# Recurrent cells at 4/3 of their pace beside a tiled feed-forward, and a first product in three float32r parts for the last two token groups

## The chip, the cores and the metric

The kernel runs on one core of a Trainium2 chip. The metric is the device time of one execution in microseconds. The engines are TensorE (PE; its weight loads are listed apart as PEld), VectorE (DVE), ScalarE (ACT), GpSimd (POOL) and SyncE (SP), which here only issues DMAs.

## The reference

An mLSTM cell runs over 768 tokens for 4 batches of 8 heads with head dimension 40. Its output, laid out as 3072 tokens of 320 values, goes through a feed-forward block with a leaky ReLU. All is float32.

```python
for t in range(S):                                   # S = 768, state C: 40x40 a head, n: 40
    m_new = max(f_gate[t] + m, i_gate[t])
    f_stab, i_stab = exp(f_gate[t] + m - m_new), exp(i_gate[t] - m_new)
    C = f_stab * C + i_stab * outer(v[t], k[t])
    n = f_stab * n + i_stab * k[t]
    y[t] = sigmoid(o_gate[t]) * (C @ q[t]) / max(abs(n . q[t]), 1)
x = y as (4 * 768, 320)
h = x @ w_in                                          # 320 -> 2048
out = max(0.01 * h, h) @ w_out                        # 2048 -> 320
```

## The kernel before

**Cells.** The 768 tokens are cut into six chunks of 128. A cell is one chunk of one batch; cell s is batch s % 4 of chunk s // 4, so there are 24. Cells of chunks 2 to 5 take two units on TensorE: `u_parts(s)` (scores of q and k and the state's additions into banks `sd`, L614 and L619; the scores are multiplied by the gate weights w on VectorE, L624, and the state gets its addition, L596) and `u_mix(s)` (one product `pT` with values and state, L695; then on VectorE transposes, a denominator, the output gate, on GpSimd L592 and L709, and a transpose L713; the result goes to a DRAM scratch `x_dr`, L716). Before `u_parts` the cell's w must be there: the gate sums of a chunk are written to the DRAM scratch `a_dr` and spread over partitions by a DMA (`spread`, L413; a second spread `ea` for q, L421), then GpSimd adds a causal mask (`prep_mask`, L450), then ScalarE takes 8 exponentials (`prep_exp`, L458). `ahead(s)` prepares k and q (loads of `rb`, L398, VectorE L505 and L511), the state (L592) and the scaled keys (L478). `feed(s + 4)`, called behind `u_mix(s)`, asks for the k, v and w of the cell that takes over its tiles (L356, L359, L413).

**Feed-forward.** A group is the 512 tokens of one chunk in all batches; there are groups 0 to 5. `gather_x` brings `x_dr` into `xT` (L730). The first product makes 16 tiles of 128 hidden units by 512 tokens, in eight pairs. A pair runs two tiles side by side on the two 64-row halves of TensorE, in five slots of 64 input rows each (L759, 10 matmuls of 512 columns); ScalarE applies the leaky ReLU on the way to `acts` (L767). The second product uses seven block products in place of eight, for two halves n, 14 products of 8 matmuls with 160 columns (L835), in the order p1, p2, p6, p7, p4, p5, p3, each for both n. The results are combined by VectorE (L853, L858, L862, L870, L887, L892), ScalarE (L854, L867, L875, L881) and GpSimd (L868, L876, L882): p4's result is added on GpSimd (L882), p5's and p3's on VectorE (L887, L892). PSUM has four banks for the products (`psf`) and four for the cells (`psc`).

**Order.** The order on TensorE, VectorE, ScalarE and GpSimd is written out by hand. Beside group g's feed-forward units (16 for the first product, 14 for the second) stand the cells of chunk g + 1, at fixed unit numbers:

```python
pairs = (2, 2, 6, 6, 14, 14, 19, 19, 19)     # u_parts x2, u_mix x2, u_parts x2, u_gates, u_mix x2
masks = {0: (2, 3), 12: (4, 5)}              # prep_mask of cells c * 4 + n ahead of unit 0 and 12
```

All DMAs but a few at the start are issued by SP, in an order made by the framework. Each engine works off its list in order, and a wait holds what is behind it. Tiles of the cells (`kn`, `qn`, `S`, `rb`, `xb` and the work tiles) live in the same pools as the rest for the whole run. `narrow_weights` (L247 to L263) works on raw weights at the start; its rows are prices of single VectorE operations.

Of the kernel before, what the change touches and what calls it, by code (L numbers as in the profile page):

```python
# [9 lines left out]
F32 = mybir.dt.float32  # L10
U32 = mybir.dt.uint32
U64 = mybir.dt.uint64
# [6 lines left out]
def kernel(  # L19
# [58 lines left out]
    dr = ctx.enter_context(tc.tile_pool(name="dr", bufs=1, space=bass.MemoryType.DRAM))  # L78

# [39 lines left out]
    kn = consts.tile([P, NL, H, DP], F32, name="kn")  # L119
    qn = consts.tile([P, NL, H, DP], F32, name="qn")  # L120
    S_t = [consts.tile([P, 2, H, DP], F32, name=f"S{n}") for n in range(NL)]
    S_v = [t[:].rearrange("p u h (k d) -> p u h k d", d=QW) for t in S_t]
    rb_t = [consts.tile([P, 3, RW], F32, name=f"rb{n}") for n in range(NR)]
    xb = consts.tile([P, PR * TB, QW], F32, name="xb")
# [147 lines left out]
    def gates(c):  # L272
# [5 lines left out]
        F = wk.tile([n, P], F32, name="F", bufs=1)  # L278
        nc.vector.tensor_tensor_scan(F[:], fc, zeros[:n].to_broadcast([n, P]), 0.0, op0=ALU.add, op1=ALU.add)
        if c > 0:  # L280
            il_t = wk.tile([BH, P], F32, name="il", bufs=1)
            nc.vector.tensor_scalar(il_t[:], il, scalar1=m0[:], scalar2=None, op0=ALU.subtract)
            il = il_t[:]
        m = wk.tile([n, P], F32, name="m", bufs=1)
        nc.vector.tensor_tensor_scan(m[:], fc, il, -1e30 if c == 0 else 0.0, op0=ALU.add, op1=ALU.max)
        a = wk.tile([n, P], F32, name="a", bufs=1)
        nc.vector.tensor_tensor(a[:], F[:], m[:], op=ALU.subtract)
        bu = wk.tile([BH, 3, P], F32, name="bu", bufs=1)
# [13 lines left out]
    def gates_exp(c):  # L302
# [9 lines left out]
        if c > 0:  # L312
            nc.sync.dma_start(a_dr[c, 0].rearrange("u n t -> n u t"), a[:].rearrange("n (u t) -> n u t", u=2))
            if c > 1:
                nc.sync.dma_start(a_dr[c, 1].rearrange("u n t -> n u t"), bu[:, 2, :].rearrange("n (u t) -> n u t", u=2))
            if 1 < c < NB - 2:
                load_fi(c + 2)
# [25 lines left out]

    def load(s):
# [11 lines left out]
        nc.sync.dma_start(d["k"][:, :, :D], k[b, :, rows, :].rearrange("h p d -> p h d"))  # L356
        for u in range(2):
            for i in range(2):
                nc.sync.dma_start(  # L359
                    S_v[n][ts(u, SL), u, :, i, :DB],  # L360
                    v[b, :, c * P + u * SL : c * P + (u + 1) * SL, DB * i : DB * (i + 1)].rearrange("h p d -> p h d"),
                )
# [42 lines left out]

    def spread(s):
# [3 lines left out]
        w = wk.tile([P, H, P], F32, name="w", bufs=NL)  # L410
        d["w"] = w[:].rearrange("p h t -> p (h t)")[:, : H * SL].rearrange("p (h t) -> p h t", t=SL)
        for u in range(2):
            nc.sync.dma_start(d["w"][ts(u, SL)], a_dr[c, 0, u, b * H : (b + 1) * H, :].partition_broadcast(SL))  # L413

    def spread_q(s):
# [3 lines left out]
        d["ea"] = wk.tile([P, H, SL], F32, name="ea", bufs=EAB)  # L419
        for r in range(2):  # L420
            nc.sync.dma_start(  # L421
                d["ea"][ts(r, SL)], a_dr[c, 1, 1 - r, b * H : (b + 1) * H, :].partition_broadcast(SL),
            )

    def spread_first(a, s2):
# [12 lines left out]
        for n in range(2):  # L438
            w = st[s2 + n]["w"] = wk.tile([P, H, P], F32, name="w", bufs=NL)
# [20 lines left out]
    def prep_vu(s):  # L460
# [3 lines left out]
        if s < NS:  # L464
            d["vu"] = wk.tile([P, H, 2, V1], F32, name="vu")
# [34 lines left out]
    def prep_kq(s):  # L500

        d = st[s]
        d["kqT"] = wk.tile([P, 2, PR * P], F32, name="kqT")
# [20 lines left out]
    def u_split(s):  # L524

        d = st[s]
        d["kqT"] = wk.tile([P, 2, PR * P], F32, name="kqT")
# [14 lines left out]
    def u_transpose(s):  # L542
        d = st[s]
        d["kqT"] = wk.tile([P, 2, PR * P], F32, name="kqT")
# [92 lines left out]
    def u_values(s):  # L637
# [4 lines left out]
        d["den"] = wk.tile([P, H], F32, name="den")  # L642
        denominators(d["den"][:], pa[:, :, D])

    def gate(s):

        d = st[s]
        d["x"] = wk.tile([P, Dm], F32, name="x")
# [7 lines left out]
    def u_plain(s):  # L656
# [13 lines left out]
        den = wk.tile([P, H], F32, name="den")  # L670
        denominators(den[:], hN[:, :, 0, DB])
        if b < 2:
            d["x"] = wk.tile([P, Dm], F32, name="x")[:]
# [10 lines left out]
    def u_mix(s):  # L684
# [16 lines left out]
        hb = wk.tile([P, PR * TB, QW], F32, name="hb", bufs=1)  # L701
        nc.vector.transpose(hb[:].rearrange("p (j n) d -> p j n d", n=TB), in_blocks(pT[:]))  # L702
        den = wk.tile([P, PR * TB], F32, name="den")
# [8 lines left out]
        xq = wk.tile([P, PR * P], F32, name="x")  # L712
# [6 lines left out]
    def gather_x(s):  # L719

        c, b = divmod(s, B)
        if ("xT", c) not in st:
            st["xT", c] = wk.tile([P, KC, GT], F32, name="xT", bufs=1)
        xT = st["xT", c]
        src = x_dr[s].rearrange("(k p) t -> p k t", p=DP)
        for r in range(2):
            at = 0
            while at < KC:
                k0, n = run_of(r, at)
                nc.sync.dma_start(xT[DP * r : DP * (r + 1), at : at + n, ts(b, P)], src[:, k0 : k0 + 2 * n - 1 : 2, :])  # L730
                at += n

# [20 lines left out]
    def ff_units(g):  # L753
        xT = st["xT", g]
# [59 lines left out]
        return firsts + fast_units(g)  # L814
# [104 lines left out]
    def ahead(s):  # L919

        if s < NS:
            if s < 2 * B:
# [99 lines left out]
    with tc.manual_schedule(engines={E.PE, E.DVE, E.Activation, E.Pool}):  # L1022
# [20 lines left out]
        for c in range(1, NB + 1):  # L1043
            if c > 1:
                ffs = ff_units(c - 1)
            cells = cell_units(c) if c < NB else []
            n_ff, n_c = len(ffs), len(cells)
            done = fed = 0
            waiting, after = [], []
            for i in range(n_ff):  # L1050
                if c == 1:
                    run(now, 2 if i < 10 else 3 if i < 14 else 4)
                    for n in fetch.get(i, ()):
                        load_weights(QN + n)
                    if i == 0:
                        prep_mask(B)
                        ahead(B)
                        load_fi(3)
                for s, steps in lazy.items():
                    if s in late and late[s] > 0:  # L1060
                        late[s] -= 1
                    else:
                        run(steps, 3)
                for n in masks.get(i, ()) if 1 < c < NB else ():
# [70 lines left out]
```

## Time and profile before

| | us |
|---|---|
| median of 3 runs (lowest, highest) | 511.85 (510.85, 513.27) |
| span of the profiled execution | 508.0 |
| the runs' median over that span (what lies around it) | 3.85 |
| PE busy | 492.0 |
| DVE, ACT, POOL busy | 308.1, 171.5, 137.7 |
| DMA queue of SP, share of 16 DMA engines | 52.2% |

The times come from executions that are not profiled; the page and the trace are of one profiled execution. Busy times are unions of an engine's instructions; DMA issues are not counted as busy, neither on SP nor on ACT. In a row by stage the columns are PE, PEld, DVE, ACT, POOL (busy us, instructions), the granted TensorE clock, the DMA share and GB/s. In the chain of waits each line has its start, its length and what it is; in a timeline, start, length, engine, line, operation, and in brackets the idle time before it and who ended it.

### The profile page before, as it was taken

The page shows a single profiled execution, that of the slowest core. Times are in us where ns is not written, and L with a number is a line of the kernel's source. Part 1 is how long each engine was busy: PE and PEld are TensorE (multiplying, and loading weights), DVE is VectorE, ACT ScalarE, POOL GpSimd, SP SyncE. Part 2 cuts the span into 40 slices and gives each one's busy share as a digit, 9 for nine tenths or more (in the row PEclk, how much of TensorE's full clock was granted, in tenths as well). Part 3 has the DMA queues.
Part 4 walks back from the last instruction along what each step waited for, and adds up shares of the span by engine and source line. Part 5 has one row for each costly group of instructions (what it writes and reads, how often), then busy time and mean ns, then how long its engine had stood idle before and what let it go on. Part 6 is the DMA issues. An engine that isn't in the chain of part 4 may idle for free.

```text
span 508.0 us, 12526 instructions
## 1 busy us (share of the span) xinstructions
PE 492.0 (97%) x4981; PEld 366.6 (72%) x4981; DVE 308.1 (61%) x515; ACT 171.5 (34%) x478; POOL 137.7 (27%) x175
## 2 busy tenths in 40 slices
PE   8878999999999999999999999999899999999997
PEld 7766878767655489955589855599755599744797
DVE  4779898899954778635765826764825664101321
ACT  3664864652722510323411323311213411022210
POOL 4243443360402404413104614014612003000020
PEclk9877999999999999999999999999999999999999
DMA  9977687888765551565663566564466212200001
GB/s 116 146 204 154 149 219 185 168 152 175 155 145 87 131 124 46 133 130 144 147 132 92 115 137 170 137 141 97 109 135 177 68 53 62 69 1 1 1 1 52
DMA packets 165290, 59.21 MB, mean 117 GB/s; under 512 B 128816, under 2 KB 156016, under 8 KB 165232
## 3 DMA queue, kind: packets, MB, share of 16 engines
q1 hardware_dynamic: 164848, 58.28, 52.2%
q8 instruction: 39, 0.64, 0.5%
q14 instruction: 19, 0.16, 0.1%
q10 hardware_dynamic: 384, 0.13, 0.1%
HBM read 51.68 MB, written 6.70 MB: 115 GB/s over the span
## 4 chain that ended last, share of the span: by engine, by line
PE 79%; DVE 9%; DMA 3%; ACT 3%; POOL 2%; issue 2%; SPq 2%; ACTq 0%; POOLq 0%; DVEq 0%
PE ph L759 36%; PE po L835 26%; PE po L794 6%; PE pT L695 3%; PE sd L614 3%; SPq L359 1%; PE sd L619 1%; DMA S<-in_v_dram 1%; ACT kqT L540 1%; PE tkq L548 1%; DVE raw L261 1%; DMA rb<-in_q_dram 1%; DMA w<-a_dr 1%; PE pa L641 1%; DVE qn L511 1%
## 5 line engine op out<-in xcount | busy, mean ns | idle before, releaser
L759 PE MATMUL ph<-xT,w_in 64*128 64x512 f32 (+1 forms) x1120 | 216.2, 538 | 2.4 <-DVE y L887 1.4
L759 PEld LDWEIGHTS ph<-xT,w_in 64*128 64x128 f32 x1120 | 108.6, 189 | 95.1 <-issue 86.3
L767 ACT ACTIVATE acts<-ph 128x512 f32<-128x512 f32 (+1 forms) x112 | 53.9, 533 | 179.0 <-PE ph L759 178.9
L835 PEld LDWEIGHTS po<-w_out,acts 128*128 128x128 f32 x640 | 87.3, 190 | 3.8 <-issue 3.8
L835 PE MATMUL po<-w_out,acts 128*128 128x160 f32 x640 | 89.1, 300 | 0.0
L450 POOL TENSOR_TENSOR w<-w,i 128x512 f32<-128x512 f32 x20 | 26.9, 1345 | 117.3 <-DMA w<-a_dr 117.2
L624 DVE TENSOR_TENSOR qn<-w,sd 64x512 f32<-64x512 f32 x40 | 27.4, 684 | 40.2 <-PE sd L619 20.5
L458 ACT ACTIVATE w<-w,gT 128x64 f32<-128x64 f32 (+1 forms) x192 | 50.8, 348 | 2.7 <-POOL w L450 1.7
L592 POOL TENSOR_TENSOR S<-S,f 40x336 f32<-40x336 f32 x36 | 32.0, 889 | 67.3 <-PE pT L695 36.3
L835 PE MATMUL po<-raw,acts 128*128 128x160 f32 x320 | 45.5, 300 | 0.0
L835 PEld LDWEIGHTS po<-raw,acts 128*128 128x128 f32 x320 | 43.9, 190 | 0.3
L794 PE MATMUL po<-w_out,acts 128*128 128x320 f32 x128 | 36.5, 436 | 0.0
L702 DVE STREAM_TRANSPOSE hb<-pT 128x512 f32<-128x512 f32 x16 | 11.5, 717 | 31.0 <-PE pT L695 30.8
L794 PEld LDWEIGHTS po<-w_out,acts 128*128 128x128 f32 x128 | 23.6, 190 | 9.3 <-issue 0.3
L511 DVE TENSOR_TENSOR qn<-kqT,ea 64x512 f32<-64x512 f32 x32 | 28.4, 888 | 1.0
L709 POOL TENSOR_TENSOR xb<-xb,den 128x320 f32<-128x320 f32 x16 | 11.7, 729 | 56.8 <-DVE xb L706 56.6
L596 DVE TENSOR_TENSOR S<-S,sd 40x336 f32<-40x336 f32 x36 | 18.1, 503 | 12.1 <-POOL S L592 11.2
L614 PEld LDWEIGHTS sd<-kqT 40*64 40x64 f32 x640 | 19.9, 135 | 6.1 <-issue 6.1
L822 DVE TENSOR_TENSOR raw<-acts 128x1024 f32<-128x1024 f32 x10 | 11.8, 1222 | 18.3 <-ACT acts L767 18.2
L713 DVE STREAM_TRANSPOSE x<-xb 128x512 f32<-128x512 f32 x16 | 18.2, 1140 | 7.6 <-POOL xb L709 7.6
L835 PE MATMUL po<-raw 128*128 128x160 f32 x160 | 22.5, 299 | 0.0
L835 PEld LDWEIGHTS po<-raw 128*128 128x128 f32 x160 | 22.0, 190 | 0.0
(151 smaller groups left out, 551.8 us busy)
## 6 DMA issues: line engine op xcount, KB each, us to landing
w<-a_dr SPq DMA_DIRECT2D x40, 128.0 KB
rb<-in_k_dram SPq DMA_DIRECT2D x64, 80.0 KB
rb<-in_q_dram SPq DMA_DIRECT2D x64, 80.0 KB
rb<-in_o_gate_dram SPq DMA_DIRECT2D x64, 80.0 KB
ea<-a_dr SPq DMA_DIRECT2D x32, 128.0 KB
kn<-in_k_dram SPq DMA_DIRECT2D x24, 160.0 KB
raw<-in_moe_w_out_dram SPq DMA_DIRECT2D x6, 640.0 KB
S<-in_v_dram SPq DMA_DIRECT2D x80, 40.0 KB
```

What stands on the lines that cost most here:

```text
L450: nc.gpsimd.tensor_tensor(w, w, cm2.unsqueeze(1).to_broadcast([P, H, SL]), op=ALU.add)
L458: yield nc.scalar.activation(w[:, h, :], w[:, h, :], AF.Exp, bias=gT[c][:, 0, bh : bh + 1], scale=1.0)
L511: nc.vector.tensor_tensor(mixed(s)[rows, 1 - r], d["kqT"][rows, 1].rearrange("p (h t) -> p h t", t=SL), d["ea"][rows], op=ALU.mult,)
L592: nc.gpsimd.tensor_tensor(new, old, g, op=ALU.mult)
L596: nc.vector.tensor_tensor(new, new, st[s]["dC", u], op=ALU.add)
L614: nc.tensor.matmul(bank[1 - u][toks, h, :], lhsT=kqT[rows, 0, ts(h, SL)], rhs=kqT[rows, 1, ts(h, SL)], start=True, stop=True,)
L624: nc.vector.tensor_tensor(mixed(s)[toks, u], w[toks], bank[1 - u][toks], op=ALU.mult)
L713: nc.vector.transpose(in_blocks(xq[:]), xb[:].rearrange("p (j n) d -> p j n d", n=TB))
L759: nc.tensor.matmul(ph[r][:, cols], lhsT=w_row(r, slot, j), rhs=xT[DP * r : DP * (r + 1), slot, cols], start=(slot == 0), stop=(slot == KC ...
L767: nc.scalar.activation(acts[:, f, cols], ph[r][:, cols], AF.Prelu, alpha=0.01)
L794: nc.tensor.matmul(po[n][:], lhsT=acts[:, f, ts(n, P)], rhs=w_out[:, f, :], start=(f == 0), stop=(f == NF - 1),)
L835: nc.tensor.matmul(bank[:], lhsT=left[:, f, :], rhs=right[:, f, :], start=f == 0, stop=f == KH - 1)
```

## The change

- The cells run by a clock of ticks, 30 a group, that goes on at 4/3 of a tick for each feed-forward unit. `pairs` and `masks` now count in ticks. Chunk 2 still begins at unit 2 of group 1; the last mix, of chunk 5, comes at unit 22 of group 3 in place of unit 19 of group 4.
- For cells of chunks 3 to 5, k and the four parts of v are asked for by ScalarE, one or two a unit, and so are all gathers of x. `spread` and `spread_q` are one DMA each in place of two.
- The cells' tiles have pools of their own, which are closed behind the last mix. In their place come three versions of `w_in` (the raw bits, a low part scaled by 2^12, and a combination of both), and the same of x.
- Group 4 from its third pair on and all pairs of group 5 make the first product as three float32r products (raw, low, dif) and combine them. The parts are made in 20 steps, two or three a unit, from unit 22 of group 3 on; those of group 5's x during group 4's second product.

```diff
-        for u in range(2):
-            nc.sync.dma_start(d["w"][ts(u, SL)], a_dr[c, 0, u, b * H : (b + 1) * H, :].partition_broadcast(SL))
+        spread_rows(d["w"], a_dr[c, 0, :, b * H : (b + 1) * H, :])
...
+        def bring(eng):
+            eng.dma_start(d["k"][:, :, :D], k[b, :, rows, :].rearrange("h p d -> p h d"))
+            yield
+            for u in range(2):
+                for i in range(2):
+                    eng.dma_start(
+                        S_v[n][ts(u, SL), u, :, i, :DB],
+                        v[b, :, c * P + u * SL : c * P + (u + 1) * SL, DB * i : DB * (i + 1)].rearrange("h p d -> p h d"),
+                    )
+                    yield
+        if c < 3:
+            for _ in bring(nc.sync):
+                pass
+        else:
+            later[s] = [bring(nc.scalar), 5]
...
-                nc.sync.dma_start(xT[DP * r : DP * (r + 1), at : at + n, ts(b, P)], src[:, k0 : k0 + 2 * n - 1 : 2, :])
+                nc.scalar.dma_start(xT[DP * r : DP * (r + 1), at : at + n, ts(b, P)], src[:, k0 : k0 + 2 * n - 1 : 2, :])
...
+    def open_parts():
+        cells_stack.close()
+        kp = ctx.enter_context(tc.tile_pool(name="kp", bufs=1))
...
+    def split_w_parts(n, half):
+        at = ts(half, WC // 2)
+        src = w_in[:, n, at]
+        held = []
+        def first():
+            t = tmp_part()[:].rearrange("p k t -> p (k t)")
+            held.append(t)
+            top_bits(t, src)                                        # VectorE, 128x640, & 0xFFFFF000
+            nc.gpsimd.tensor_tensor(t, t, src, op=ALU.subtract)
+        def second():
+            t = held[0]
+            nc.vector.scalar_tensor_tensor(
+                parts["w", "dif"][n][:, at], in0=t, scalar=1.0 + 1.0 / EPS, in1=src, op0=ALU.mult, op1=ALU.add,
+            )
+            nc.scalar.activation(parts["w", "low"][n][:, at], t, AF.Copy, scale=1.0 / EPS)
+        return first, second
+    def split_x(s):
...
+        top_bits(t, src)
+        nc.vector.tensor_tensor(low, t, src, op=ALU.subtract)
+        nc.vector.scalar_tensor_tensor(
+            parts["x", "dif"][:, :, cols], in0=low.bitcast(F32), scalar=1.0 + 1.0 / EPS, in1=src, op0=ALU.mult, op1=ALU.add,
+        )
...
+        def triple(j):                                              # rows(): 5 slots x 2 halves, float32r
...
+            def first():
+                ph.extend(psf.tile([P, GT], F32, name=f"ph{r}", tag="mm") for r in range(2))
+                rows(j, ph, "raw", True, False)
+            def second():
+                rows(j, ph, "low", False, True)
+            def third():
+                pe.extend(psc.tile([P, GT], F32, name=f"pe{r}", tag="c") for r in range(2))
+                rows(j, pe, "dif", True, True)
+                fs = [acts[:, f_of(r, j), :] for r in range(2)]
+                for r in range(2):
+                    nc.scalar.activation(fs[r], pe[r][:], AF.Copy, scale=-EPS)
+                for r in range(2):
+                    nc.vector.scalar_tensor_tensor(
+                        fs[r], in0=ph[r][:], scalar=1.0 + EPS, in1=fs[r], op0=ALU.mult, op1=ALU.add,
+                    )
+                for r in range(2):
+                    nc.scalar.activation(fs[r], fs[r], AF.Prelu, alpha=0.01)
...
+            order = [steps[0][0], steps[1][0], steps[0][1], steps[2][0], steps[1][1], steps[3][0], steps[2][1], xs[0], xs[1]]
+            order += [steps[4][0], steps[3][1], xs[2], xs[3]]
+            for m in range(5, len(steps)):
+                order += [steps[m][0], steps[m - 1][1]]
+            return order + [steps[-1][1]]
...
+        for g in range(1, NB):
+            firsts, seconds = three_units(g, LEAD if g == THREE[0] else 0) if g in THREE else ff_units(g)
+            ffs = firsts + seconds
+            at.update(group=g, past=False)
+            for i in range(len(ffs)):
+                at["past"] = i >= len(firsts) - 1
+                upto = min(ENDS + 1, (TICKS * (g - 1) + i + 1) * 4 // 3)
+                for m in range(t, upto):
+                    before_tick(m)                                  # exponentials, masks
                 ffs[i]()
...
+                for m in range(t, upto):
+                    after_tick(m)                                   # cells, ahead, load_late, feed
+                gather()
+                if t <= ENDS < upto:
+                    open_parts()
+                    for n in range(QN):
+                        fetch_w_part(n)
+                    todo = split_steps()
+                t = max(t, upto)
+                bring_later(1 if i < len(firsts) else 2)
+                prepare(3 if i < len(firsts) else 2)
+                if g + 1 < NB and g in THREE and i in range(len(firsts) + 4, len(firsts) + 12, 2):
+                    split_x((g + 1) * B + (i - len(firsts) - 4) // 2)
```

## The prediction

> **What bounds the kernel now.** I read the page first, its busy times and then its chain, and after that the chain in order of time from 139 us on, the busy times by stage, and the timelines of SP and POOL around two mixes. The page:
>
> ```profile
> PE 492.0 (97%) x4981; PEld 366.6 (72%) x4981; DVE 308.1 (61%) x515; ACT 171.5 (34%) x478; POOL 137.7 (27%) x175
> ```
>
> TensorE is busy all the time, so a gain must come out of its work. The chain of waits in order of time shows where that work stands:
>
> ```profile
> 159.31 17.37 PE ph L759 x80
> ...
> 344.26 3.33 DMA w<-a_dr
> ...
> 347.74 1.24 POOL w L450
> ...
> 365.26 7.59 PE ph L759 x31
> ...
> 439.79 34.53 PE ph L759 x160
> 474.33 30.64 PE po L835 x224
> ```
>
> From 139 us on the chain is TensorE, but for one stretch, 341.5 to 365.3 us: a load of w (the spread gate sums of a cell) comes late, POOL's mask addition (L450) waits for it, everything queued on POOL and VectorE behind that is late, and TensorE idles 1.4 us at 365.3. Group 5, free of cells, gives clean prices: 34.53 us for eight pairs of the first product, 4.316 us a pair; 2.19 us for each of 14 products of the second. The busy times by stage (groups 1, 2 and 5; each first product, then second):
>
> ```profile
> 139.40:180.60 41.20, 41.20 (x481) 21.01 (x481) 25.51 (x38) 13.38 (x37) 10.48 (x11) 1.00 0.57 124
> 180.60:214.20 33.60, 33.60 (x298) 33.15 (x296) 23.74 (x39) 8.07 (x28) 10.79 (x14) 1.00 0.39 91
> 214.20:255.50 41.30, 41.30 (x481) 21.02 (x481) 23.13 (x43) 12.95 (x36) 8.83 (x10) 1.00 0.61 144
> 439.80:474.30 34.50, 34.50 (x161) 15.37 (x161) 2.68 (x3) 7.60 (x14) 0.00 (x0) 1.00 0.02 6
> ```
>
> PE is full in each; DVE (third) has room, 49 of 75 us. SP is not counted there, so its timeline, behind the mix of cells 12 and 13 (PE pT, 232.04 to 234.05):
>
> ```profile
> 237.15 5.40 SPq L716 DMA_DIRECT2D x_dr<-x  x8
> ...
> 255.61 0.43 SPq L356 DMA_DIRECT2D kn<-in_k_dram  x1
> 256.14 3.01 SPq L359 DMA_DIRECT2D S<-in_v_dram  x4
> 259.20 1.77 SPq L413 DMA_DIRECT2D w<-a_dr  x2
> ...
> 263.60 2.69 SPq L359 DMA_DIRECT2D S<-in_v_dram  x4
> 266.33 1.40 SPq L413 DMA_DIRECT2D w<-a_dr  x2
> ```
>
> SP issues without a break, some 0.45 us apiece, and asks for the second w only 33 us after that mix. POOL's timeline shows who pays:
>
> ```profile
> 263.49 1.27 POOL L450 TENSOR_TENSOR w<-w,i 128x512 f32<-128x512 f32 x1 [19.95 <-DMA w<-a_dr]
> 270.95 1.27 POOL L450 TENSOR_TENSOR w<-w,i 128x512 f32<-128x512 f32 x1 [6.20 <-DMA w<-a_dr]
> ```
>
> POOL stands 20 us for a load. It costs nothing here because this falls in a first product, where POOL owes TensorE nothing (0.00 in group 5's row).
>
> **The change, part by part.** *The first product.* Six pairs of group 4 and eight of group 5 become three float32r products. No row shows a float32r matmul. Group 5's 160 records are two for each f32 matmul, 216 ns apiece with two row halves side by side: one slot of both halves takes 34.53/40 = 863 ns. Below, three products in place of the four (high and low part of each operand) that a full one needs: 863/4 = 216 ns, 15 of them 3.24 us a pair, 14 x 1.08 = 15.1 us gained. Above, a float32r product costs a whole f32 record on each half: 432 ns, 6.48 us a pair, 30.3 us lost. I take 216, an estimate: the change's own arithmetic needs a product that reads one part of each operand, and an f32 record of 432 ns must hold two such streams. The Trainium skill ("FP8 and Floating Point Precision", TensorE Precision Notes) says that true FP32 takes four passes and that a reduced form truncates the operands; by that the gain is the same 15.1 us. The extra evacuation hides: per pair ACT 4 x 0.59 = 2.4 us and DVE 2 x 0.68 = 1.4 us (L624's row for PSUM) under 3.24 us of PE, with PSUM banks for two pairs; uncovered, it would be one tail.
>
> *The pace.* The cells' matmuls are the same; they only come sooner. Of DVE's 49 us a group some 12 are feed-forward (2.7 + 9.3 beside group 5), so it goes to 37 x 4/3 + 12 = 61 of 75: covered on the mean, but in bursts. A gain is excluded: TensorE waited for the cells 1.4 us in all. So I follow the worst queue, where the old stall sits. In the new order, the mix of cells 16 and 17 stands behind the fifth of group 2's 14 second products; the masks of 20 and 21, whose w is asked for only after that mix, stand ahead of the ninth; on POOL the two additions of the ninth and tenth products (L882) queue behind the masks, on DVE the additions of the eleventh (L887) behind those, and behind them the multiplications (L624) that release the PSUM banks and let the next mix go. From the end of the mix: SP begins 3.1 us later (237.15 - 234.05) and runs to the second w in 30.6 us; k and v go to ScalarE (-0.43-3.01-0.43-2.69 = -6.6), two ea and two w issues merge (-2.7): 21.3 us. Landing 3.3, mask 1.3: 29.0 us. Then L882 1.3, L887 0.6, two cells of L624 and L596 3.8: 34.7 us. TensorE has nine products and two short pieces for that time: 19.7 + 2.0 + 1.7 = 23.4 us. **Stall 11.3 us.** Bounds: with SP at a bare 0.45 us for its 31 issues it is 14.0 in place of 21.3, stall 4; if SP also waits on ScalarE's transfers (the eight completion counters are shared by the two queues, and an issue waits for the counter's last user) 15.
>
> *The split.* Twenty steps stand between the last mix (cells 22, 23, behind group 3's seventh product) and group 4's first triple. Their tiles take the cells' memory, so they wait for the last x store: 9.5 us after the mix (417.86, stores issued to 425.95, landing 1.41). Fourteen steps are on DVE ahead of the last product's addition: six bit masks of 0.50 (L259's median), four second steps of 0.83 (L261's), four cells of x at 2.2, with six additions 17 us: 26.5 us. TensorE has seven products and one pair, 19.6 us, before it needs that bank: 6.9 us. Each second step also waits for a POOL subtraction of 1.46 to 1.92 us (twice L709's 0.73 or L478's 0.96): 7 to 13, I take 11.
>
> *ScalarE's issues.* 36 a chunk leave SP for ACT at 0.6 us (L730, L359), 20 us; ACT has room on the mean (13.4 and 8.1 us busy a stage). But 25 stand in a row between group 1's last Prelu and the first copy of the fifth product: 15.3 us of issue where TensorE needs 11. Prelus, PSUM copies and the exponentials for the next multiplication queue behind them. Four banks absorb most: 0 (issue runs beside the ACT pipe) to 8, I take 6 over groups 1 to 3.
>
> *The clock.* After short idles early on, the granted clock is 0.50 from 21.0 to 31.2 and from 38.0 to 44.8 us. A stall of 11 us should cost one such window: half of 6.8, 3.4 us. The Trainium skill ("TensorE: Matmul & The Clock Gate", Part 1) says that an idle window of some 3.4 us halves the clock; the trace agrees in kind, with shorter idles.
>
> The sum on the profiled execution: 508.0 - 15.1 - 1.4 (the old stall) + 11.3 + 11 + 6 + 3.4 = 523.2 us. Its own median is 511.85, 3.85 more than the span: **527 us**.
>
> **The rivals.** *Hidden after all (faster).* If w of cells 20 and 21 is masked by 17.7 us after the mix (29.0 - 11.3), POOL is free before TensorE asks, and if DVE has slack for the split, only 4 us of stalls stay: 508.0 - 16.5 + 4 + 3.85 = 499 us. For it: SP loses 36 issues a chunk, the x gathers too, and DVE was idle for a third of these stages. Against: the rows above put 8 stores and 18 loads ahead of the first w. *float32r dear (slower still).* At 432 ns a slot, 527 + 45.4 = 572 us. For it: two records for each f32 matmul may mean one stream each; or a weight load (189 ns in L759's row) lies in line: 216 + 189 = 405. Against: in the second product 16 records take 2.19 us, 137 ns each, and each has a 128-column load under it. The Trainium skill (the clock's page, Part 3) lets loads overlap running matmuls only in another row group, by which it would be near 572; the second product, one row group, disagrees. *In between.* Stalls of 14 to 19 us in place of 31.7 eat the gain up: 510 to 514 us.
>
> **How the numbers follow.** Forecast 0.69, dear float32r 0.11, hidden 0.14, in between 0.06. Range 506 to 546: from a half-hidden stall to both stalls at their upper bounds (15 + 13 in place of 22.3, ACT's 8 in place of 6) with a second slow clock window and 5 us more; it leaves out float32r's 0.11 and part of the hidden case. A measurement tells 0.5% (2.6 us) from no change: faster 0.14, same 0.06, slower 0.80. The forecast's own range is 515 to 546.
>
> **What would show it.** Right: a float32r slot at 216 ns; POOL's mask waiting for w near the end of group 2 with PE idle some 11 us just before group 3; DVE full of split steps at the start of group 4 with PE waiting for banks; the clock at 0.50 after the first. Wrong: PE at 97% or more through groups 1 to 4, or group 5's first product not near 26 us.

## The result and the profile after

The changed kernel takes 632.94 us in the median (630.17 to 634.12, four runs), the kernel before 511.35 us beside it: a ratio of 1.237 with a 95% interval of 1.2313 to 1.2427. Slower was right; 527 us and the range 506 to 546 were wrong by 106 us. The profiled execution took 631.95 us with a span of 630.2 us. One execution each of e1, e9, e13, e15 and e17 was slow: the ratios below leave it out, the medians hold it and are up to 1.4 us higher for it, and the traces of e1 and e15, taken in such an execution, are not read (e19_two_loads_again is e1's kernel once more).

The page of the changed kernel, its busy line and the clock granted to TensorE in 40 slices:

```profile
PE 513.2 (81%) x5121; PEld 409.4 (65%) x5121; DVE 358.5 (57%) x583; ACT 194.2 (31%) x514; POOL 155.2 (25%) x183
PEclk9689889996997987999697986579999889999999
```

TensorE was idle for 16.0 us before (508.0 - 492.0) and is idle for 117.0 now (630.2 - 513.2): 101 of the 122 us. The other 21 are busy time: 12 us fewer of float32r work, and 33 us more. Of these 33, 28 are the clock: TensorE is busy for 72.1 us while the granted clock is 0.50, against 15.9 us before, and half of the difference is lost. Where the other 5 come from no view shows. So the question is what TensorE waits for. Its timeline, the largest wait, and the five small ones where group 4 begins (start, duration, line, and in brackets the idle time before it with what ended it):

```profile
412.04 0.39 PE L333 MATMUL tg<-ident,bu 32*128 32x32 f32 x2 [34.11 <-DVE S L631]
...
488.80 4.61 PE L979 MATMUL po<-w_out,acts 128*128 128x160 f32 x32 [1.84 <-ACT hn L1025]
497.91 1.30 PE L903 MATMUL ph<-xT,w_in 64*128 64x512 f32 x2 [4.50 <-DVE y L1031]
501.23 6.69 PE L903 MATMUL ph<-xT,w_in 64*128 64x512 f32 x20 [2.01 <-DVE y L1031]
508.82 4.56 PE L903 MATMUL ph<-xT,w_in 64*128 64x512 f32 x18 [0.90 <-DVE y L1036]
514.92 1.33 PE L840 MATMUL ph<-xT,w_raw 64*128 64x512 f32 x5 [1.54 <-issue]
```

The first is the forecast's stall at the end of group 2, three times its size. The five others are its second stall, 10.8 us for 11. Four further rows of TensorE's waits (engine, line, releaser, us in total, times, longest) have 45.4 us that the forecast did not have:

```profile
PE ph L903 <- ACT acts L911: 16.5, 4, 10.1
PE po L979 <- ACT y L1011: 10.2, 1, 10.2
PE po L938 <- DVE w_out L267: 10.0, 2, 9.1
PE po L979 <- ACT acts L911: 8.7, 2, 4.9
```

The chain of waits in order of time says what the first stall is made of:

```profile
378.09 8.23 DMA ea<-a_dr
...
389.29 12.10 DMA w<-a_dr
401.46 1.26 POOL w L485
```

The load of w takes 12.10 us. Before, the one on the same chain took 3.33 us. POOL's timeline shows the mask behind it:

```profile
401.46 1.26 POOL L485 TENSOR_TENSOR w<-w,i 128x512 f32<-128x512 f32 x1 [33.27 <-DMA w<-a_dr]
```

The slow loads reach further than their own readers. SP's waits have these rows (L430 loads q, k and the output gate, L751 stores x):

```profile
SPq L430 <- DMA ea<-a_dr: 18.8, 7, 4.1
SPq L430 <- DMA w<-a_dr: 14.0, 4, 6.0
SPq L751 <- DMA w<-a_dr: 11.9, 3, 5.3
```

None of these requests reads ea or w. But all 455 requests of SP and 132 of ScalarE in this trace report their landing to the same eight completion counters (semaphores), and a request waits until the last user of its counter has landed.

The chain's end, at 568.55 us and on, gives the float32r price: two products and then the third of one pair, 20 and 10 records.

```profile
568.55 2.52 PE ph L840 x20
571.07 1.13 PE pe L840 x10
572.20 2.32 PE ph L840 x20
574.52 1.13 PE pe L840 x10
```

2.32 + 1.13 = 3.45 us a pair, or 230 ns for each of 15 slots, where the f32 pair took 4.316 us. Eight pairs make 27.6 us, near the 26 of the forecast.

### The profile page after: what moved, and what is told of

Read it like the earlier page. It is cut to its first block, busy times and chain, and to the rows that moved or that the text cites. A ratio compares the mean times of both kernels' runs of the same rounds, so it can differ in the third digit from the quotient of the medians.

```text
span 630.2 us, 12882 instructions
## 1 busy us (share of the span) xinstructions
PE 513.2 (81%) x5121; PEld 409.4 (65%) x5121; DVE 358.5 (57%) x583; ACT 194.2 (31%) x514; POOL 155.2 (25%) x183
## 4 chain that ended last, share of the span: by engine, by line
PE 44%; DMA 23%; SPq 11%; DVE 11%; issue 5%; POOL 3%; ACT 2%; ACTq 1%; DVEq 0%; POOLq 0%
PE po L979 15%; PE ph L903 12%; DMA w<-a_dr 6%; DMA S<-in_v_dram 6%; PE ph L840 6%; SPq L233 5%; PE po L938 4%; DMA ea<-a_dr 3%; PE pe L840 3%; SPq L430 2%; DMA rb<-in_k_dram 2%; DMA xT<-x_dr 2%; PE pT L730 2%; DMA raw<-in_moe_w_out_dram 2%; PE sd L649 1%
## 5 line engine op out<-in xcount | busy, mean ns | idle before, releaser
L903 PE MATMUL ph<-xT,w_in 64*128 64x512 f32 (+1 forms) x840 | 166.3, 543 | 23.9 <-ACT acts L911 16.5
L903 PEld LDWEIGHTS ph<-xT,w_in 64*128 64x128 f32 x840 | 94.7, 200 | 84.7 <-issue 48.1
L979 PE MATMUL po<-w_out,acts 128*128 128x160 f32 x640 | 97.1, 314 | 10.6 <-ACT acts L911 8.7
L979 PEld LDWEIGHTS po<-w_out,acts 128*128 128x128 f32 x640 | 93.9, 201 | 14.4 <-ACT acts L911 9.1
L911 ACT ACTIVATE acts<-ph 128x512 f32<-128x512 f32 (+1 forms) x84 | 38.6, 511 | 99.1 <-PE ph L903 84.2
L485 POOL TENSOR_TENSOR w<-w,i 128x512 f32<-128x512 f32 x20 | 29.9, 1500 | 131.0 <-DMA w<-a_dr 123.8
L979 PEld LDWEIGHTS po<-raw,acts 128*128 128x128 f32 x320 | 45.7, 196 | 14.6 <-ACT y L1011 10.7
L1012 POOL TENSOR_TENSOR y<-y,raw 128x160 f32<-128x160 f32 x10 | 8.2, 827 | 131.0 <-ACT y L1011 105.2
L938 PEld LDWEIGHTS po<-w_out,acts 128*128 128x128 f32 x128 | 24.9, 202 | 20.8 <-DVE w_out L267 11.0
L1031 DVE TENSOR_TENSOR hn<-hn,po 128x160 f32<-128x160 f32 x10 | 3.2, 316 | 59.1 <-POOL hn L1026 36.6
L862 DVE SCALAR_TENSOR_TENSOR acts<-ph,acts 128x512 f32<-128x512 f32 x28 | 18.0, 686 | 29.7 <-ACT acts L860 29.7
L333 PE MATMUL tg<-ident,bu 32*128 32x32 f32 x13 | 2.0, 238 | 34.6 <-DVE S L631 34.1
L529 ACT ACTIVATE rb<-rb 128x320 f32<-128x320 f32 x20 | 8.8, 468 | 65.7 <-DMA rb<-in_o_gate_dram 65.7
L649 PE MATMUL sd<-kqT 40*64 40x64 f32 x640 | 23.4, 227 | 5.0 <-DVE kqT L540 5.0
L631 DVE TENSOR_TENSOR S<-S,sd 40x336 f32<-40x336 f32 x36 | 18.1, 503 | 14.8 <-POOL S L627 13.7
```

Source lines behind the costliest of these rows:

```text
L485: nc.gpsimd.tensor_tensor(w, w, cm2.unsqueeze(1).to_broadcast([P, H, SL]), op=ALU.add)
L649: nc.tensor.matmul(bank[1 - u][toks, h, :], lhsT=kqT[rows, 0, ts(h, SL)], rhs=kqT[rows, 1, ts(h, SL)], start=True, stop=True,)
L903: nc.tensor.matmul(ph[r][:, cols], lhsT=w_row(r, slot, j), rhs=xT[DP * r : DP * (r + 1), slot, cols], start=(slot == 0), stop=(slot == KC ...
L911: nc.scalar.activation(acts[:, f, cols], ph[r][:, cols], AF.Prelu, alpha=0.01)
L938: nc.tensor.matmul(po[n][:], lhsT=acts[:, f, ts(n, P)], rhs=w_out[:, f, :], start=(f == 0), stop=(f == NF - 1),)
L979: nc.tensor.matmul(bank[:], lhsT=left[:, f, :], rhs=right[:, f, :], start=f == 0, stop=f == KH - 1)
```

## The experiments

Times are medians; the kernel before took 509.5 to 510.7 us beside them. In kernels with two loads the lines after L440 have numbers lower by two (L485 is L483).

**Two loads in place of one (e1_two_loads).** The changed kernel asks for w and for ea in one request of 128 partitions each, with the source read as 2 x 64 rows.

```diff
-        nc.sync.dma_start(to.rearrange("p h t -> p (h t)"),
-            rows.unsqueeze(1).to_broadcast([2, SL, H, SL]).rearrange("u p h t -> u p (h t)"))
+        for u in range(2):
+            nc.sync.dma_start(to[ts(u, SL)], rows[u].partition_broadcast(SL))
```

> Changed kernel, but each w and each ea is asked for in two loads of 64 partitions again, as in the kernel before; all else as changed. Theory M (the merged load of 128 partitions is slow by itself, 12.1 to 12.7 us from issue to landing against 3.3 us for one half before, and every stall stands behind one): w lands in 3 to 4 us again, the 34.1-us stall before group 3 falls to 10 or less, the time falls by 90 to 115 us to 515 to 545. Theory Q (ScalarE's queue: its issues of k, values and gathers of x wait for transfers and hold up the Prelus and copies behind them): little change, 600 to 635. Theory P (only the pace and the place of the masks): 610 to 640, SP has even more issues.

545.61 us, ratio 1.066 (1.0605 to 1.0718): 87 us of the loss of 122 hang on this one edit. Theory M holds as the main cause, and Q and P fall; but M's stall of 10 us or less did not come true (18.2 us in e19).

**ScalarE's issues back to SP, without and with that edit (e2_sp_queue, e3_two_sp).**

```diff
-            later[s] = [bring(nc.scalar), 5]
+            later[s] = [bring(nc.sync), 5]
...
-                nc.scalar.dma_start(xT[DP * r : ...
+                nc.sync.dma_start(xT[DP * r : ...
```

> Changed kernel, but k, values and gathers of x are asked for by SP instead of ScalarE; the merged loads stay. M: w still lands in some 12 us, the time stays above 590, and may get worse since SP has 36 issues more a chunk. Q: the ScalarE waits (L911, L1011, L998: some 40 us of TensorE's idle time) go, 570 to 595. P: 630 to 650.

640.36 us (ratio 1.254, 1.2482 to 1.2595), 7 us worse; theory Q had 570 to 595.

> Both edits: two loads again, and k, values and gathers of x asked for by SP. What stays is the pace, the split steps and the float32r products. M: near the first run, 515 to 545, a few us either way for ScalarE's issues. Q: clearly below both others. P: above 600.

548.15 us (1.0735, 1.0696 to 1.0775), near e1. At this pace the total hardly changes with the queue that asks; the stall does (25.2 us here, 18.2 in e19), and e19 shows why.

**The merged load alone, put into the kernel before (e5_before_merged).** Only w, not ea.

```diff
-        for u in range(2):
-            nc.sync.dma_start(d["w"][ts(u, SL)], a_dr[c, 0, u, b * H : (b + 1) * H, :].partition_broadcast(SL))
+        nc.sync.dma_start(d["w"].rearrange("p h t -> p (h t)"),
+            a_dr[c, 0, :, b * H : (b + 1) * H, :].unsqueeze(1).to_broadcast([2, SL, H, SL]).rearrange("u p h t -> u p (h t)"))
```

> Kernel before with one edit: each w is asked for in one load of 128 partitions in place of two of 64 (ea stays in two). M: w lands in some 12 us in place of 3.3, masks come some 8 us later, and at the place where TensorE waited 1.4 us it now waits for 5 to 12 us in each of groups 1 to 3: 520 to 545. Q and P: no change or a gain from fewer issues, 508 to 513.

544.13 us (1.065, 1.0603 to 1.0696), 34 us slower with 20 requests fewer. The waits (engine, line, releaser, total, times, longest) and the chain of this kernel (its L452 is the mask addition, L450 in the kernel before):

```profile
POOL w L452 <- DMA w<-a_dr: 153.9, 12, 28.5
```

```profile
286.78 8.53 DMA w<-a_dr
```

POOL waited 117.2 us for w in the kernel before.

**Is it the size of the request or how its source is written? (e12_outer2)** Two requests of 64 partitions, as in e1, but each source written as 2 x 32 rows.

```diff
-            nc.sync.dma_start(to[ts(u, SL)], rows[u].partition_broadcast(SL))
+            nc.sync.dma_start(to[ts(u, SL)].rearrange("p h t -> p (h t)"),
+                rows[u].unsqueeze(0).unsqueeze(0).to_broadcast([2, SL // 2, H, SL]).rearrange("a p h t -> a p (h t)"))
```

> Changed kernel with two loads each for w and ea as in the first run, same bytes and same number of requests, but the source of each is written as 2 x 32 rows in place of 64 (the same row, step 0, in both dimensions). Theory (the outermost dimension of the source sets over how many DMA engines a request is spread, and 2 is slow): each load takes about half of the merged one's time, 6 to 7 us, and the two lie together; the time is 580 to 640, near the changed kernel. Rival (128 partitions, or 256 KB in one request, is what is slow): w lands in 3 to 4 us, 541 to 550 as in the first run.

642.66 us (1.257, 1.2495 to 1.2646): as slow as the merged load, with the bytes, the requests and the partitions of e1. Its chain:

```profile
292.86 7.54 DMA ea<-a_dr
301.38 7.66 DMA ea<-a_dr
310.91 11.91 DMA w<-a_dr
333.37 8.20 DMA w<-a_dr
```

So the request is slow because its source begins with a dimension of 2, not because it is large. The Trainium skill ("DMA: Bandwidth & Descriptors", Why a DMA increments its semaphore by 16 and not by 1) says that the number of DMA engines of a request is the largest one up to 16 that divides the slowest dimension of both sides: 2 here, 16 for 64 rows. The time agrees, and so do the steps in which the completion counters rise in the traces. Each of the 36 loads of w and ea in the changed kernel, and each of the 72 in e12, raises its counter in three steps: one at once and two when data land (0.92, 11.98 and 12.10 us after the request for the w above). Each of the 72 loads from 64 rows in e19 raises it in 16 steps, all as data land. The same page of the Trainium skill (Rules for kernel authors) advises one 128-partition transfer in place of two halves; written like this the measurement says the opposite, by 87 us.

**The first stall, step by step (e19_two_loads_again).** The kernel of e1, for its trace.

> The same kernel as the first run, two loads each for w and ea, for its trace: a span of 539 to 545, the wait before group 3 at 17 to 21 us (18.5 us in the f32 variant of it), in which the second w is asked for over 30 us after the end of the mix of cells 16 and 17, where the prediction had 21.3.

549.44 us in the one run, span 547.6. SP, POOL and TensorE around the stall:

```profile
288.34 4.52 SPq L430 DMA_DIRECT2D rb<-in_k_dram  x4
292.96 3.70 SPq L430 DMA_DIRECT2D rb<-in_q_dram  x4
298.54 1.78 SPq L441 DMA_DIRECT2D ea<-a_dr  x2
...
301.97 3.63 SPq L749 DMA_DIRECT2D x_dr<-x  x8
...
321.43 1.09 SPq L441 DMA_DIRECT2D w<-a_dr  x2
```

```profile
325.26 1.26 POOL L483 TENSOR_TENSOR w<-w,i 128x512 f32<-128x512 f32 x1 [2.06 <-DMA w<-a_dr]
```

```profile
329.55 0.39 PE L333 MATMUL tg<-ident,bu 32*128 32x32 f32 x2 [18.18 <-DVE S L629]
```

The mix of cells 16 and 17 ends at 289.3. SP starts its stores 12.6 us later (3.1 in the forecast), because requests of the cells before still stand there, four of them taking 4.52 us where four took some 1.9; from there to the second w it is 20.6 us (21.3, with the merge), the masks are done 4.0 us later (4.6), TensorE starts 3.0 us after (5.7), and TensorE's list lasted for 22.0 us (23.4). So the second w is asked for 33.2 us after the mix, where the prediction had 3.1 + 21.3 = 24.4 (the 21.3 above counts from SP's start). The stall is 18.2 where 11.3 was forecast, and the start of SP is the step that was wrong. SP does not stand there for lack of time alone; among its waits from 274 to 302 us are these:

```profile
SPq L430 <- DMA xT<-x_dr: 3.9, 3, 2.6
SPq L441 <- DMA xT<-x_dr: 3.4, 2, 2.9
SPq L430 <- DMA S<-in_v_dram: 2.6, 3, 1.0
SPq L441 <- DMA kn<-in_k_dram: 1.8, 1, 1.8
```

These 11.7 us go to gathers, values and k that ScalarE asked for, through the shared counters; SP's loads here (k, q and ea) read none of them. The prediction had this case as the upper bound of its stall, 15 us. In e3 SP asks for everything: it issues without a break from 258 to 327 us, starts its stores 20.5 us after the mix, and the stall is 25.2 us. So SP is late either way, once by waiting for ScalarE's transfers and once by its own list.

**The masks behind the second products (e6_masks_late).**

```diff
-            for n in masks.get(i, ()) if c < NB else ():
+            for n in masks.get({12: -1, 20: 12}.get(i, i) if c == 4 else i, ()) if c < NB else ():
```

> Two loads each for w and ea as in the first run, and the masks of cells 20 and 21 are put eight ticks later, behind group 2's second products in POOL's queue (first unit of group 3). Theory A (the prediction's first stall: POOL's masks wait for w ahead of the additions of the ninth and tenth second products, VectorE's additions and the release of the PSUM banks stand behind them; 25.2 us of TensorE's idle time before group 3 and some 13 us of half clock behind it in the run with both edits): both go, and 10 to 15 us at most come back in group 3, where the late exponentials of these cells are needed: 515 to 530. Rival (the wait only moves: SP is that late for every load behind it, so group 3's first multiplications wait as long): 538 to 546.

530.41 us (1.039, 1.0322 to 1.0454), 15 us less, just past the outer end of what theory A gave. The wait before group 3 is gone. One of 5.8 us stands in group 3 instead: TensorE waits for ScalarE's Prelus (L909), these stand behind its `prep_o` (L527), and that waits for SP's load of the output gate. SP is late for the next request too.

**The float32r products away (e7_f32).** `THREE = ()`, nothing split.

> Two loads each for w and ea; groups 4 and 5 keep the four-pass f32 first product, so no operand is split and no part of w is loaded again; pace and ScalarE's queue as changed. If the float32r part is worth what the trace of the changed kernel shows (3.45 us a pair against 4.32, 12 us gained; 10.7 us of waits on the split and a half clock of 3 to 5 us behind it lost), the time stays within 5 us of the first run: 541 to 550. If the split costs much more than these waits: below 535. If it costs nothing: 555 to 560. The stall before group 3 must still be there, 20 to 26 us.

541.06 us (1.059, 1.0532 to 1.0645): 4.5 us less without float32r than with it, though the two intervals overlap, so that a loss by float32r is not shown. The matmul gain of 12 us was spent: the split's waits are 9.8 us in e19, and the clock falls behind them.

**The split put later (e13_late_split),** on e6: HOLD is 10 units, LEAD 4, and the parts of `w_in` for n = 2 and 3 go first.

```diff
-                prepare(3 if i < len(firsts) else 2)
+                prepare((2 if i < 8 else 1) if i < len(firsts) else int(i >= len(firsts) + HOLD))
```

> The run with two loads and late masks (530.4 us), with the split put later: its first step four units after the last mix instead of right behind it, one step a unit, the weights' parts for group 4 first, and four of group 4's pairs instead of two in f32 (two pairs fewer gain 0.87 us each). The prediction's second stall (10 us of waits on VectorE's additions at the start of group 4, and 5 us of half clock behind them) should go, 1.7 us are lost: 514 to 520. Rival (the split's work itself is too much for VectorE there, wherever it stands): 526 to 534.

521.45 us (1.025, 1.0162 to 1.0329), 9 us less, just outside the expected 514 to 520. The five waits are gone. A new one stands behind the first two triples, where TensorE needs the banks that VectorE's combination of the first (L860) frees:

```profile
417.21 2.25 PE L838 MATMUL ph<-xT,w_raw 64*128 64x512 f32 x7 [2.48 <-DVE acts L860]
```

**The cells at the old pace (e9_pace1_f32, e8_pace1_g5, e11_gather_sp).** One tick a unit, on e1; e9 has `THREE = ()`, e8 has `THREE = (NB - 1,)` (six of group 5's pairs), e11 is e9 with the gathers of x, and these alone, on `nc.sync`.

```diff
-                upto = min(ENDS + 1, (TICKS * (g - 1) + i + 1) * 4 // 3)
+                upto = min(ENDS + 1, TICKS * (g - 1) + i + 1)
```

> As the run before this, with f32 products in group 5 too: what is left of the change is that k, values and gathers are asked for by ScalarE and spread over the units, and the cells' pool. The prediction's term for ScalarE's issues is 6 us: 510 to 518. If they hide: 506 to 511. If ScalarE's waits for transfers count: 520 or more.

530.52 us (1.038, 1.031 to 1.0441): some 19 us over the kernel before, for what the forecast priced at 6. TensorE's waits in this kernel, and ScalarE's timeline around one of them:

```profile
PE po L977 <- ACT y L1009: 15.3, 7, 3.0
```

```profile
359.64 3.97 ACTq L763 DMA_DIRECT2D xT<-x_dr  x4
...
365.34 0.29 ACT L1009 COPY y<-po 128x160 f32<-128x160 f32 x1 [12.73 <-DMA xT<-x_dr]
```

The chain has the first of the four stores that these gathers read; ScalarE stood until they had landed:

```profile
356.85 1.35 DMA x_dr<-x
```

ScalarE stands 12.7 us in gathers of x and in the wait for their stores, and the copy that frees a PSUM bank stands behind them.

> Two loads each for w and ea; the cells at the pace of before (one tick a unit, done in group 4), and only group 5 with float32r products (six of its eight pairs); ScalarE's queue as changed. Theory A: at this pace the masks stand where they stood before, so the 20 to 25-us stall is gone; the gain is six pairs at 0.87 us, 5 us; the split has ten units of group 4 before it is needed and waits some 3 us: 504 to 514. Rival (ScalarE's issues or the merged gate stores cost by themselves): 515 to 530.

539.47 us (1.057, 1.0524 to 1.0614). Above both ranges: with ScalarE's issues and the early split, float32r cost some 9 us here instead of gaining 5.

> Pace 1, f32 products, two loads for w and ea as in the run at 530.5 us, but the gathers of x go back to SP; k and values stay with ScalarE. In that run TensorE waits in every second product (2 to 4 us) for ScalarE's copy of the fifth and sixth products (L1009), with eight gather issues of 0.6 us apiece ahead of it on ScalarE. Theory (the gathers hold up the copies): the waits go, 508 to 514. Rival (k and values on ScalarE, or waits for a shared completion counter): 520 to 531.

509.40 us (0.997, 0.9939 to 0.9998). The gathers alone were some 20 us; k and values on ScalarE, one or two requests a unit, cost nothing that shows at this pace.

**Only the pace (e18_pace_only).** e11 at 4/3 of the pace, with the late masks.

> Two loads, late masks, gathers of x on SP, f32 products everywhere: against the run at 509.4 us only the pace of the cells is 4/3 and three masks stand later. If the pace itself is what still costs (SP or VectorE cannot follow the cells in bursts): 522 to 532. If the pace is free once loads and masks are right, and what is left was ScalarE's gathers and the split: 508 to 514.

536.73 us (1.0515, 1.0455 to 1.0575). Above both ranges: the pace costs 27 us when SP does the gathers. TensorE's waits:

```profile
PE ph L901 <- ACT acts L909: 14.9, 2, 13.6
PE ph L901 <- DMA xT<-x_dr: 9.6, 1, 9.6
```

Ahead of the longer one, at 336.46 us, SP's timeline runs from 300.95 us through 13 gathers and three gate stores to the first store of x at 312.83, and the output gate that ScalarE needs before its Prelus lands 20 us after that. SP has the requests of e11 and three quarters of the time. But it waits as well. The chain of that wait has, right ahead of SP's gathers, a transfer that ScalarE asked for, and SP's waits from 284 to 303 us hold 11.8 us for such transfers; the chain's line and the two largest waits:

```profile
297.99 4.49 DMA S<-in_v_dram
```

```profile
SPq L441 <- DMA S<-in_v_dram: 4.7, 1, 4.7
SPq L430 <- DMA kn<-in_k_dram: 4.7, 1, 4.7
```

Which part of the 27 us is SP's own issuing and which these waits, no run separates.

**Three looks at what is left at the faster pace (e15_thin, e17_pace65) and at the slower (e14_g5_split, e16_needed).** e15 is e13 with two gather requests a unit (`gather_x` yields after each), and one of k or values.

```diff
-                gather()
+                gather(4 * 8 if i == len(ffs) - 1 else 2)
...
-                bring_later(1 if i < len(firsts) else 2)
+                bring_later(1)
```

> The run with two loads, late masks and late split (521.5 us), with the gathers of x spread on ScalarE at two issues a unit instead of four, and k and values at one a unit throughout. If bursts on ScalarE make the waits for its copies and Prelus (0.7 + 0.9 + 2.0 + 0.7 + 1.9 us and a half clock behind two of them): 513 to 518. If SP's lateness makes them: 519 to 523.

521.55 us (1.021, 1.0159 to 1.0252), no change: at this pace the bursts of gathers are not what is left.

e17 is e15 at 6/5, with LEAD 6, and with every mask kept out of eight units of the second products (18 to 25) in place of the one late pair:

```diff
-                upto = min(ENDS + 1, (TICKS * (g - 1) + i + 1) * 4 // 3)
+                upto = min(ENDS + 1, (TICKS * (g - 1) + i + 1) * 6 // 5)
...
+            while due and not (c < 5 and NF + 2 <= at["unit"] < NF + 10):
+                prep_mask(due.pop(0))
```

> Two loads, thin gathers on ScalarE, late split, cells at 6/5 of the pace (done at group 4's second unit), masks kept out of the first ten units of the second products, float32r in two of group 4's pairs and all of group 5's (8.7 us gained). If SP's issues were the bound at 4/3 (their time is 0.9 of a chunk's 56 us there, 0.8 of 62 us here): 502 to 510. If not: 512 to 520.

527.91 us (1.035, 1.0308 to 1.0382), not better. Its waits were new ones on VectorE (7.3 us at L1000, 5.7 at the split of x, 5.3 at L1029). Since the kernel moved masks, split and gathers together, it does not tell whether the slower pace helped SP.

e14 is e11 with float32r in four of group 5's pairs (`THREE = (NB - 1,)`, `LEAD = 4`) and the late split of e13; e16 also leaves out the halves of the weights that those four pairs never read. From e14 to e16:

```diff
-            for m in range(0, 4):
-                order += [steps[m][0]] + ([steps[m - 1][1]] if m else [])
-            return order + [steps[3][1]]
+            return order
...
-                    for n in range(QN):
+                    for n in (2, 3):
                         fetch_w_part(n)
...
-                prepare((2 if i < 8 else 1) if i < len(firsts) else int(i >= len(firsts) + HOLD))
+                prepare(1 if i < len(firsts) else int(i >= len(firsts) + HOLD))
```

> Pace 1, two loads, gathers of x on SP, float32r in four of group 5's pairs, the split late as in the run before. If ScalarE's gathers and the split were what cost there (539.5 us with both): 505 to 512, four pairs gain 3.5 us on the run with f32 and gathers on SP. If the split still stalls TensorE: above 515.

509.29 us (0.998, 0.995 to 1.0001): the gain of 3.5 us was eaten by a wait of 2.5 us, again behind the first two triples for L860, and a half clock behind it.

> Pace 1, two loads, gathers on SP, float32r in four of group 5's pairs (509.3 us), with only the halves of the weights that these pairs use loaded and split (12 steps in place of 20, one a unit). The 2.5-us wait at the first triple and the half clock behind it (1.7 us) should go: 504 to 508, some 1% under the kernel before. If the split costs by its mere presence: 508 to 511.

505.61 us (0.993, 0.9896 to 0.9959): faster than both kernels. Its page, and its chain from the last f32 pairs through the first triple:

```profile
PE 488.3 (97%) x5021; PEld 371.9 (74%) x5021; DVE 327.7 (65%) x543; ACT 179.3 (36%) x490; POOL 143.9 (29%) x179
```

```profile
435.95 17.37 PE ph L901 x80
453.31 2.33 PE ph L838 x20
455.64 1.14 PE pe L838 x9
```

TensorE does not wait between them, nor for any later triple: the split is hidden at last, and 3.8 us against e11 are left of it (four pairs at 0.87 make 3.5).

## Why the prediction was wrong

*The failed step: the merge of the loads.* In the first stall's sum "two ea and two w issues merge (-2.7)" and "Landing 3.3" stand side by side. The 3.3 us belonged to a request of 64 partitions; the change gave SP another request, whose cost no row showed, and it was booked as a saving. It measured 8.2 us for ea and 8.4 us for w in the median, 12.1 us for the w of the first stall, and 87 us in all: every w and ea that is loaded so comes late, and requests of SP that share their counters wait with them (44.7 us in the three rows above). float32r, which no row showed either, was bounded from both sides; this edit was not. That the mechanism goes by the source's first dimension is shown by e12.

*The first stall* stood where it was forecast, with the chain that was forecast (w, POOL's masks, the additions, the release of the banks): 34.1 us in the changed kernel, 18.2 with two loads, 11.3 forecast, upper bound 15. What was short is SP's start, 12.6 us after the mix where the trace of before had 3.1. In e19 it waited 11.7 us for transfers that ScalarE had asked for; with all requests on SP (e3) it is its own list that is late. The sum took SP's start from a kernel in which neither was the case, and kept the shared counters for the upper bound; the steps behind the start were forecast too long by 4.0 us, which hid a part. The lower bound (4) counts 31 issues where the rows have 36.

*The pace* was "covered on the mean, but in bursts", by VectorE's busy time. The engine that comes late is SP: 27 us in e18, by its issues and by its waits for ScalarE's transfers. Both were counted for one stretch and not for a whole chunk.

*ScalarE's issues and the old stall*: 6 - 1.4 us forecast. With two loads at the new pace all of TensorE's further idle time over the kernel before is 4.8 us (e19: 48.8 - 16.0 less the two stalls of 18.2 and 9.8), close to the forecast. That these are ScalarE's issues is not shown: in e3, where SP asks for all, the same sum leaves 3.3 us (55.2 - 16.0 less 25.2 and 10.7). At the old pace the same gathers cost some 20 us (e9 against e11): there the stores of x that they read are made only then (ScalarE waits 6.6 to 9.6 us for the first of them in each chunk), and the engine that must free the banks stands waiting. At the new pace no gather of e19 waits over 1 us for a store. The forecast counted 0.6 us of issue apiece and no wait.

*The split*: 11 us forecast, 10.8 measured; VectorE's additions release 7.4 of it, as forecast, a ScalarE copy 1.8, and for 1.5 no releaser shows. The 11 was taken from a span of 7 to 13, so the match to 0.2 us is luck. e13 took most of it away with the steps later and two float32r pairs fewer.

*float32r*: 216 ns a slot forecast, 230 measured, 12.1 us gained for 15.1 (14 pairs times 4.316 - 3.45). The dear rival (432 ns) is excluded, and a weight load does not lie in line.

*The clock*: 3.4 us forecast, for one window. The busy time is longer by 33 us, 513.2 - (492.0 - 12.1), of which 28 fall into half clock; with two loads by 19, of which 16 do (4 of them in the first 54 us, long before the stalls named here). Behind its first 54 us the changed kernel has twelve stretches of half clock with 55.3 us of work in them, a loss of 2.3 us apiece. The size of one was near and the count was not.

With two loads the forecast's sum of 523.2 stands against a span of 547.6 (e19). The 24.4 us between them are the busy time (15.5), the first stall (6.9) and float32r (3.0), less 1.0 for the split and the rest; 523.2 itself stood on the merge's saving of 2.7, which no run shows. Some of it is this one execution: e1, the same kernel, had spans of 539.7 to 543.9. The upper end of the range, 546, is 543 by its own terms. What stays open is the last 11 us at 4/3 of the pace: e13 and e15 have float32r's gain, late masks and a late split, and still take 521 us. That SP's lateness makes them is likely by e18 (in e13 SP waits some 13 us for ScalarE's transfers between 274 and 302 us) and was not shown: e17 mixed several edits, and no run has the faster pace, late masks and all requests on SP.

## What to carry to other kernels

Price a merged request as a new operation, and look at the first dimension of both of its sides before counting the issue that it saves: here one request in place of two cost 87 us. Before work is packed closer in time, add up the requests that its queue must issue in that time for the whole stage, not for the one stretch under the eye. Requests that wait for another transfer belong on an engine for which nothing waits: on ScalarE, the gathers that SP carried for nothing cost some 20 us. A second queue does not free the first where both report to the same completion counters: look in the first queue's waits for transfers of the second.

## What the hardware showed

A load whose source begins with a dimension of 2 landed in 7.2 to 13.7 us (36 loads of the changed kernel, median 8.4 for w and 8.2 for ea). In e12, with half the bytes, the median was 8.4 and 7.2 us; the same bytes from a source of 64 rows landed in 3.2 and 3.4 us (72 loads of e19). Its completion counter rose in 3 steps, and in 16 for 64 rows. SP and ScalarE share eight such counters, and SP waited 11.7 us in 28 for ScalarE's transfers (e19). The clock falls to half after short waits in a busy stretch: in e9 two waits of 2 to 3 us, at 365.7 and 370.1, were followed by a window at half clock (a row has the stretch, its length, five engines' busy times with TensorE first, and then the granted clock).

```profile
369.50:372.50 3.00, 2.37 (x13) 2.38 (x14) 0.00 (x0) 0.58 (x3) 1.04 (x2) 0.80 0.84 137
372.50:390.00 17.50, 17.50 (x104) 13.27 (x105) 1.75 (x6) 5.68 (x21) 6.95 (x9) 0.94 0.67 148
```

0.80 over 3.0 us and 0.94 over 17.5 us make 3.3 us at half clock, after 5 us of waiting in all. And a float32r slot with two row halves side by side takes 230 ns where the f32 slot takes 863, 3.75 times as long.
